# An attention and expert kernel on one core: the short chunk of the second pair moves to the end, and one PSUM bank is borrowed in the first twelve steps

## The chip, the core and the metric

The kernel runs on one core of a Trainium2 chip. The metric is device time in microseconds, the median of a few executions of the whole program, with nothing done on the host between. Lower is better. TensorE (PE), VectorE (DVE), ScalarE (ACT), GpSimd (POOL) and the DMA queue of SyncE (SP) each work through a list of instructions in order, and wait for each other by semaphores.

## What is computed

An attention with a learned position bias, then a two-layer network with squared ReLU on its output:

```python
scores = scale * np.matmul(q, k.transpose(0, 1, 3, 2))      # 4 batches, 8 heads, 576 positions, head width 64
x = (psi_rel / psi_i)[..., None]                            # from the positions alone
bias = np.maximum(x @ w1 + b1, 0.0) @ w2                    # hidden width 32, one value per head
scores = scores + bias.transpose(2, 0, 1)[None, :, :, :]
attn = softmax(scores)
y = np.matmul(attn, v)                                      # 2304 tokens of 512
h = np.maximum(y @ moe_w_in, 0.0)                           # 512 -> 2048
out = h * h @ moe_w_out                                     # 2048 -> 512
```

## The kernel before

**Pairs, chunks, steps.** The four batches are two pairs, p = 0 and 1. The 576 query rows of a batch are cut into five chunks: c = 1 to 4 have 128 rows for each of the two batches, 256 tokens in all; c = 0 is the short one, the last 64 rows of both batches, 128 tokens in all. A step is one pair, one chunk and one head, so there are 80 steps, eight to a chunk. `ORDER` (line 40) says in which order the chunks of each pair run. In the first pair the short chunk comes first. In the second pair it comes second, as steps 48 to 55; steps 56 to 79 are three full chunks.

**A step of attention.** `qk` (line 366) makes the scores in PSUM, `softmax_a` (393) adds the bias and takes the maximum on DVE (line 405, once for each batch of a full step, once in all for a short one) and the exponentials on ACT (line 411). `softmax_b` (414) brings the exponentials into the layout that the product with v needs. For the first two chunks of the first pair, steps 0 to 15, it does this with float32 transposes on PE: four blocks of 128 columns at line 423 for each batch, then the rest block of 64 columns at line 427, each into a PSUM bank that ACT copies out (lines 424 and 428). For all later steps ACT and POOL split the exponentials into two float16 parts (lines 436 to 438) and the DMA queue transposes them (440, `at<-a`). `pv` (446) is the product with v. It stands three steps behind in the program (`LAG`).

**Banks of PSUM.** The pool `ps_h` has two banks, tag `h`, and three kinds of user: the transposes of steps 0 to 15, the bias products `bp` (line 317) and the first-layer outputs `hp` (line 524). They take its banks in the order of the program. `ps_o` has one bank each for `o0` and `o1`, the second-layer outputs; the first four bias groups and the weight conversion (`ci`, bank `o1`) also use them.

**The network.** When the eight heads of a chunk are done, `finish_x` (492) scales and splits the rows and transposes them by DMA (`xt<-xh`), and puts eight units into a queue. A unit is `g1` (515): 24 matmuls at line 524, of 256 columns for a full chunk and 128 for the short one; then relu on ACT (530), a product on DVE (532), a cast on DVE or POOL (127 or 125) and a difference on POOL (534); and `g2` (537): 12 matmuls of 512 columns at line 547 for a full chunk, 6 for the short one. `g2` of a unit follows two units behind its `g1` (`GLAG`). A step takes one unit from the queue, or two if more than `BACKLOG` wait; after step 79 the rest of the queue drains.

**The order.** The order written in the program is a wish: the Tile scheduler orders the instructions of each engine by its own model of time, so that a change in one place can move neighbours too. The position bias is made during steps 0 to 31 (`hgen`, `bias_mm`), written to a table in DRAM (`biasd`) and read back for each step (`bt`). The weights are converted in the first 16 steps.

Of the kernel before, what the change touches and what calls it, by code (L numbers as in the profile page):

```python
# [8 lines left out]
F32 = mybir.dt.float32  # L9
# [27 lines left out]
HID = "122222222211111000"  # L37

W_AT = [3, 2, 2, 2, 2, 2, 2, 2, 2, 2, 2, 2, 2, 2, 2, 1]
ORDER = [[0, 3, 2, 4, 1], [1, 0, 4, 2, 3]]  # L40
LAG, GLAG = 3, 2
BACKLOG = 10
AHEAD = 3
# [6 lines left out]
def tile_attention_moe(  # L50
# [14 lines left out]
    def pool(name, bufs, **kw):  # L65
        return ctx.enter_context(tc.tile_pool(name=name, bufs=bufs, **kw))
# [23 lines left out]
    ps_h = pool("ps_h", 2, space=PS)  # L90
    ps_o = pool("ps_o", 1, space=PS)
# [22 lines left out]
    now = [0]  # L114
# [6 lines left out]
    def cast(eng, out, in_, scale=1.0):  # L121
        if eng == "A":
            nc.scalar.activation(out=out, in_=in_, func=AF.Copy, scale=scale)  # L123
        elif eng == "P":
            nc.gpsimd.tensor_scalar(out, in_, scale, 1.0, op0=ALU.mult, op1=ALU.mult)
        else:
            nc.vector.tensor_scalar(out, in_, scale, None, op0=ALU.mult)  # L127


    k_t, v_t, q_t, v32 = {}, {}, {}, {}  # L130
    f32c = [(0, c) for c in ORDER[0][:NF]]

    def as_f32(t):
        return t.rearrange("p a b -> p (a b)").bitcast(F32)
# [279 lines left out]
    def softmax_b(p, c, h):  # L414
        e = st_.pop((p, c, h))
        nb = 2 if c else 1
        if (p, c) in f32c:

            at = as_f32(at_p.tile([128, 20, 128], F16, tag="at", name="at")).rearrange("p (k i) -> p k i", i=128)
            for b in range(nb):  # L420
                tp = ps_h.tile([128, 512], F32, tag="h", name="tp")
                for k in range(4):
                    nc.tensor.transpose(tp[:, 128 * k:128 * k + 128], e[:, S * b + 128 * k:S * b + 128 * k + 128], ident)
                nc.scalar.activation(out=at[:, 4 * b:4 * b + 4, :], in_=tp.rearrange("p (k i) -> p k i", i=128), func=AF.Copy)
            tp = ps_h.tile([128, 512], F32, tag="h", name="tp")
            for b in range(nb):
                nc.tensor.transpose(tp[0:64, 128 * b:128 * b + 128], e[:, S * b + 512:S * b + 576], ident)
            nc.scalar.activation(out=at[0:64, 4 * nb:5 * nb, :], in_=tp[0:64, 0:128 * nb].rearrange("p (k i) -> p k i", i=128),
                                 func=AF.Copy)
            st_[p, c, h, "t"] = at  # L430
            return
        a = a_p.tile([128, 2304], F16, tag="a", name="a")

        ev = e[:, 0:nb * S].rearrange("p (b j) -> p b j", b=nb)
        av = a[:, 0:nb * 2 * S].rearrange("p (b j) -> p b j", b=nb)
        cast("A", av[:, :, 0:576], ev)
        nc.gpsimd.tensor_tensor(av[:, :, 576:640], ev[:, :, 512:576], av[:, :, 512:576], op=ALU.subtract)  # L437
        nc.gpsimd.tensor_tensor(av[:, :, 640:1152], ev[:, :, 0:512], av[:, :, 0:512], op=ALU.subtract)  # L438
        at = at_p.tile([128, 20, 128], F16, tag="at", name="at")
        nc.sync.dma_start_transpose(out=at[:, 0:9 * nb, :], in_=a[:, 0:nb * 2 * S])  # L440
        st_[p, c, h, "t"] = at
# [121 lines left out]

    order = [(p, c) for p in range(2) for c in ORDER[p]]
    steps = [(p, c, h) for p, c in order for h in range(H)]
# [169 lines left out]
    for t in range(NS + LAG):  # L735
# [5 lines left out]
        if t < NS:  # L741
            p, c, h = steps[t]
            qk(p, c, h)
            softmax_a(p, c, h)
            if t + 2 < NS:
                bias_ld(*steps[t + 2])
            if h % 4 == 2 and t + 2 < NS:
                q_split(*qlist[(t + 2) // 4])
                q_next()
            if len(moe) > BACKLOG:  # L750
                moe_unit()
            softmax_b(p, c, h)
            if last < 0 or steps[last][2] != H - 1:
                moe_unit()
# [74 lines left out]
```

## Time and profile before

| | us |
|---|---|
| median of 3 runs | 669.49 (669.07 to 672.53) |
| the profiled execution, its own time | 673.4 |
| its span, first to last instruction | 671.7 |
| PE busy | 618.1 (92%) |
| DVE busy | 409.6 (61%) |
| ACT busy | 384.9 (57%) |
| POOL busy | 376.4 (56%) |

The span has two parts. In the first 190 us no engine is full: the bias, the weights and the first steps share PE, DVE, ACT, POOL and the DMA engines. From there to the end PE is busy nearly all the time, apart from some short gaps. Busy shares over the whole span hide this; they are read for each stretch.

### The profile page before, as it was taken

What the parts mean: (1) busy time and instruction counts of PE and PEld (TensorE: products, weight loads), DVE (VectorE), ACT (ScalarE), POOL (GpSimd) and SP (SyncE); (2) the same over time, 40 slices, a digit from 0 to 9 for tenths busy, and PEclk for the clock granted to TensorE, in tenths of its full rate; (3) what the DMA queues carried; (4) which work ended last, traced back from release to release, by engine and by line L of the source; (5) the groups of instructions that cost most, each with busy time, mean ns of one, the idle gap of its engine ahead of it and who ended that gap; (6) DMA issues with size and microseconds to landing.
All of it is one profiled execution on the core that took longest, in us unless ns stands there. A gap on an engine that the chain in (4) does not pass through costs nothing.

```text
span 671.7 us, 15521 instructions
## 1 busy us (share of the span) xinstructions
PE 618.1 (92%) x6048; PEld 395.1 (59%) x6048; DVE 409.6 (61%) x809; ACT 384.9 (57%) x855; POOL 376.4 (56%) x391
## 2 busy tenths in 40 slices
PE   5676689899899999999999999999997999999997
PEld 2233356566455556765666766666664776676664
DVE  7787999898854864596676443446467546424111
ACT  5588789577865655645656532556666555521111
POOL 2665569798665455766675543455565554632221
PEclk9577889799999999999999999999997999999999
DMA  6999888576978777889978976557899678451000
GB/s 232 279 276 297 269 241 242 156 230 160 208 137 188 166 167 166 191 170 220 235 153 163 174 142 117 137 94 168 159 185 214 140 131 167 107 103 32 32 1 31
DMA packets 206568, 112.16 MB, mean 167 GB/s; under 512 B 167072, under 2 KB 183456, under 8 KB 206496
## 3 DMA queue, kind: packets, MB, share of 16 engines
q1 hardware_dynamic: 206496, 111.19, 72.3%
q8 instruction: 47, 0.77, 0.5%
q14 instruction: 25, 0.20, 0.1%
HBM read 55.44 MB, written 15.61 MB: 106 GB/s over the span
## 4 chain that ended last, share of the span: by engine, by line
PE 62%; DVE 11%; DMA 11%; ACT 5%; POOL 5%; issue 4%; SPq 0%; DVEq 0%; POOLq 0%; ACTq 0%
PE o L547 22%; PE hp L524 22%; PE pv L470 6%; DMA at<-a 5%; PE sc L389 4%; DVE hg L290 3%; PE bp L317 3%; DMA biasd<-be 2%; POOL a L438 2%; DVE s L405 2%; DMA bt<-biasd 1%; ACT s L411 1%; PE sc L383 1%; DVE ci L211 1%; PE sc L377 1%
## 5 line engine op out<-in xcount | busy, mean ns | idle before, releaser
L524 PE MATMUL hp<-xt,winH 128*128 128x256 f16 (+1 forms) x1280 | 196.0, 263 | 2.6 <-DMA xt<-xh 2.2
L547 PE MATMUL o<-woutH,g 128*128 128x512 f16 x576 | 185.9, 382 | 1.4 <-ACT o L554 0.8
L524 PE MATMUL hp<-xt,winL 128*128 128x256 f16 (+1 forms) x640 | 162.4, 262 | 0.0
L524 PEld LDWEIGHTS <-winH 128*128 128x128 f16 x1280 | 117.1, 98 | 36.1 <-issue 16.0
L547 PEld LDWEIGHTS <-g 128*128 128x128 f16 x864 | 82.8, 98 | 93.2 <-issue 9.1
L532 DVE TENSOR_TENSOR r<-hp,r 128x512 f32<-128x512 f32 (+1 forms) x80 | 50.7, 634 | 135.6 <-ACT r L530 135.5
L438 POOL TENSOR_TENSOR a<-s,a 128x1024 f16<-128x1024 f32 (+1 forms) x64 | 130.2, 2034 | 0.0
L534 POOL TENSOR_TENSOR g<-r,g 128x512 f16<-128x512 f32 (+1 forms) x80 | 86.0, 1075 | 78.5 <-DVE g L127 76.5
L405 DVE CUSTOM_DVE_ANT_0 s<-sc,bt 128x576 f32<-128x576 f32 x144 | 103.5, 751 | 31.7 <-PE sc L389 22.2
L411 ACT ACTIVATE s<-s,nm 128x576 f32<-128x576 f32 x144 | 111.4, 773 | 6.8
L547 PE MATMUL o<-woutL,g 128*128 128x512 f16 x288 | 109.9, 382 | 0.0
L437 POOL TENSOR_TENSOR a<-s,a 128x128 f16<-128x128 f32 (+1 forms) x64 | 28.8, 450 | 138.3 <-ACT a L123 126.3
L409 ACT ACTIVATE nm<-mx,esc 128x1 f32<-128x1 f32 x144 | 41.3, 287 | 108.2 <-DVE mx L405 108.0
L123 ACT ACTIVATE a<-s 128x1152 f16<-128x1152 f32 (+1 forms) x64 | 70.5, 1102 | 50.9 <-DMA at<-a 49.6
L470 PE MATMUL pv<-v,at 128*128 128x64 f16 (+5 forms) x2112 | 96.8, 208 | 1.5 <-DMA at<-a 1.1
L530 ACT ACTIVATE r<-hp 128x512 f32<-128x512 f32 (+1 forms) x80 | 43.1, 539 | 57.0 <-PE hp L524 56.0
L470 PEld LDWEIGHTS <-at 128*128 128x128 f16 (+1 forms) x1792 | 58.0, 100 | 21.1 <-issue 7.7
L290 DVE TENSOR_SCALAR hg<-tab_t,nb 128x528 f32<-128x528 f32 (+17 forms) x96 | 65.4, 729 | 7.1 <-PE bp L317 6.8
L524 PEld LDWEIGHTS <-winL 128*128 128x128 f16 x640 | 62.8, 98 | 6.2 <-issue 0.4
L317 PE MATMUL bp<-hg,w2s 128*32 128x288 f32 (+17 forms) x352 | 49.0, 544 | 7.1 <-ACT hg L287 3.7
L389 PE MATMUL sc<-k,q 64*128 64x512 f16 x384 | 54.7, 390 | 0.0
L127 DVE TENSOR_SCALAR g<-r 128x512 f16<-128x512 f32 (+1 forms) x61 | 37.2, 610 | 2.4
(72 smaller groups left out, 638.4 us busy)
## 6 DMA issues: line engine op xcount, KB each, us to landing
bt<-biasd SPq DMA_DIRECT2D x64, 288.0 KB, 3.2
stg<-w_in SPq DMA_DIRECT2D x16, 512.0 KB, 5.2
stg<-w_out SPq DMA_DIRECT2D x16, 512.0 KB, 4.9
bt<-biasd SPq DMA_DIRECT2D x32, 144.0 KB, 3.5
qst<-qd SPq DMA_DIRECT2D x32, 128.0 KB, 3.4
out<-o SPq DMA_DIRECT2D x16, 256.0 KB, 2.4
v<-vd SPq DMA_DIRECT2D x8, 320.0 KB, 6.2
stg<-vd SPq DMA_DIRECT2D x8, 320.0 KB, 4.0
```

Source lines behind the costliest of these rows:

```text
L123: nc.scalar.activation(out=out, in_=in_, func=AF.Copy, scale=scale)
L290: nc.vector.tensor_scalar(ht, tab_t[:, 0:dlen(G)], scl[:, n:n + 1], nb1, op0=ALU.mult, op1=ALU.max)
L317: nc.tensor.matmul(out=bp[32 * t:32 * t + 32, 0:d1 - d0], lhsT=w2s, rhs=ts_[t][:, d0:d1], start=True, stop=True, tile_position=(0, 32 * t))
L389: nc.tensor.matmul(out=sc[:, 1024 * b:1024 * b + 512], lhsT=qt[r, qz, qs], rhs=kt[r, z, 64 * b:64 * b + 512], start=(n == 0), stop=(n == 2 ...
L405: nc.vector.tensor_tensor_reduce(s[:, 576 * b:576 * b + 576], sc[:, 960 * sb:960 * sb + 576], bt, inv, -3.0e38, ALU.add, ALU.max, mx[:, b: ...
L411: nc.scalar.activation(out=sl, in_=sl, func=AF.Exp, bias=nm[:, b:b + 1], accum_out=su[:, h, b:b + 1])
L438: nc.gpsimd.tensor_tensor(av[:, :, 640:1152], ev[:, :, 0:512], av[:, :, 0:512], op=ALU.subtract)
L470: nc.tensor.matmul(out=dst, lhsT=lhsT, rhs=vt[r, 5 * b + blk, :] if f32 else vt[:, vz, 5 * b + blk, :], start=(n == 0), stop=(n == nt - 1) ...
L524: nc.tensor.matmul(out=hp[:, f * T:f * T + T].rearrange("p (b t) -> p b t", b=nb), lhsT=wt[:, k, c0:c0 + 128], rhs=xt[:, 0:nb, z * 4 + k, ...
L532: nc.vector.tensor_tensor(rr, hp[:, 0:2 * T], rr, op=ALU.mult)
L534: nc.gpsimd.tensor_tensor(g[:, 1, 0:2 * T], r[:, 0:2 * T], g[:, 0, 0:2 * T], op=ALU.subtract)
L547: nc.tensor.matmul(out=blk["o"][b], lhsT=g[:, z, c0:c0 + 128], rhs=wt[:, 2 * u + f, :], start=(u == 0 and f == 0 and z == 0 and wt is wout ...
```

## The change

`ORDER` of the second pair becomes [1, 4, 2, 3, 0]: the full chunks 4, 2 and 3 become steps 48 to 71, and the short chunk becomes steps 72 to 79. In steps 0 to 11 the rest blocks (line 427) are written to bank `o0` of `ps_o`; steps 12 to 15 use `ps_h` as before.

```diff
-ORDER = [[0, 3, 2, 4, 1], [1, 0, 4, 2, 3]]
+ORDER = [[0, 3, 2, 4, 1], [1, 4, 2, 3, 0]]
...
-            tp = ps_h.tile([128, 512], F32, tag="h", name="tp")
+            tp = ps_o.tile([128, 512], F32, tag="o0", name="tp") if now[0] < 12 else ps_h.tile([128, 512], F32, tag="h", name="tp")
             for b in range(nb):
                 nc.tensor.transpose(tp[0:64, 128 * b:128 * b + 128], e[:, S * b + 512:S * b + 576], ident)
```

No instruction is added or taken away; what moves is shown at three places.

DVE, step 66, before: the second maximum of the step (`s,mx`), then the end of a full chunk (`x`, `ax`, `cc`, `xh`), with the product `r<-hp` and the cast `g<-r` of one unit in between.

```order
L405 ISA s,mx<-sc,bt 128x576
L405 ISA mx 128x1
L482 TENSOR_TENSOR x<-pv,rd 128x256 x2
L499 TENSOR_REDUCE ax<-x 128x2
L532 TENSOR_TENSOR r<-hp,r 128x256
L501 TENSOR_SCALAR ax<-ax 128x1 x2
L127 TENSOR_SCALAR g<-r 128x256
L502 RECIPROCAL cc<-ax 128x2
L507 TENSOR_SCALAR xh<-x,cc 128x512
L508 SCALAR_TENSOR_TENSOR xh<-x,cc,xh 128x512
```

The same step in the changed kernel:

```order
L405 ISA s,mx<-sc,bt 128x576
L405 ISA mx 128x1
L482 TENSOR_TENSOR x<-pv,rd 128x256 x2
L499 TENSOR_REDUCE ax<-x 128x2
L501 TENSOR_SCALAR ax<-ax 128x1 x2
L502 RECIPROCAL cc<-ax 128x2
L507 TENSOR_SCALAR xh<-x,cc 128x512
L508 SCALAR_TENSOR_TENSOR xh<-x,cc,xh 128x512
L532 TENSOR_TENSOR r<-hp,r 128x512
```

The unit beside this step is one of the short chunk before (256 wide) and one of a full chunk now (512 wide). It is so in each of the steps 61 to 68.

ACT, the end of the program, before: the last step's exponentials, then relus of the units and the copies of the two output banks.

```order
L411 ACTIVATE s,sum<-s,nm 128x576
L530 ACTIVATE r<-hp 128x512
L123 ACTIVATE a<-s 128x2x576
L479 ACTIVATE rd<-sum,eps 128x8
L530 ACTIVATE r<-hp 128x512 x2
L503 ACTIVATE os<-ax 128x2
L530 ACTIVATE r<-hp 128x512 x5
L554 ACTIVATE o<-o_8525,os 128x512
L554 ACTIVATE o<-o_8526,os 128x512
L530 ACTIVATE r<-hp 128x512 x6
L554 ACTIVATE o<-o_9012,os 128x512
L554 ACTIVATE o<-o_9013,os 128x512
```

The same end in the changed kernel:

```order
L411 ACTIVATE s,sum<-s,nm 128x576
L479 ACTIVATE rd<-sum,eps 128x4
L123 ACTIVATE a<-s 128x576
L530 ACTIVATE r<-hp 128x512 x3
L503 ACTIVATE os<-ax 128x1
L530 ACTIVATE r<-hp 128x512 x3
L530 ACTIVATE r<-hp 128x256 x2
L554 ACTIVATE o<-o_8582,os 128x512
L554 ACTIVATE o<-o_8583,os 128x512
L530 ACTIVATE r<-hp 128x256 x6
L554 ACTIVATE o<-o_9063,os 128x512
```

The eight short units now stand at the very end, after all attention, and the last block has one output bank instead of two.

PE, after the scores of step 9, before: the transposes of step 8 (x8, both batches), its rest blocks, a bias product, the first transposes of step 9.

```order
L389 MATMUL sc<-k,q 128x512
L423 MATMUL tp<-ident,s 128x128 x8
L470 MATMUL pv<-v,at 128x64 x4
L427 MATMUL tp<-ident,s 64x128 x2
L317 MATMUL bp<-hg,w2s 32x400 x4
L423 MATMUL tp<-ident,s 128x128 x4
L470 MATMUL pv<-v,at 128x64 x6
```

The same place in the changed kernel:

```order
L389 MATMUL sc<-k,q 128x512
L423 MATMUL tp<-ident,s 128x128 x4
L427 MATMUL tp<-ident,s 64x128 x2
L423 MATMUL tp<-ident,s 128x128 x4
L470 MATMUL pv<-v,at 128x64 x5
L317 MATMUL bp<-hg,w2s 32x400 x4
L423 MATMUL tp<-ident,s 128x128 x4
L470 MATMUL pv<-v,at 128x64 x5
```

The rest blocks at line 427 in this piece are now those of step 9, not of step 8, and stand ahead of the second half of step 8's transposes and of the bias product. Steps 9 to 11 show the same.

## Rows read from the trace of the kernel before

**Rows 1.** Stretches: start:end, length, busy of PE, PEld, DVE, ACT, POOL, PEclk, DMA, GB/s.

```profile
0.00:190.00 190.00, 149.19 (x1267) 87.56 (x1267) 160.03 (x296) 142.53 (x328) 132.49 (x158) 0.87 0.83 231
190.00:471.46 281.46, 277.91 (x2877) 179.68 (x2875) 164.23 (x329) 156.66 (x345) 159.06 (x160) 1.00 0.80 165
471.46:519.92 48.46, 42.91 (x567) 27.84 (x566) 30.48 (x68) 32.06 (x74) 28.18 (x28) 0.93 0.94 190
519.92:668.10 148.18, 148.07 (x1345) 100.01 (x1342) 54.83 (x116) 52.97 (x108) 56.68 (x48) 1.00 0.41 82
...
384.00:436.80 52.80, 52.80 (x558) 35.12 (x556) 22.59 (x48) 20.61 (x47) 24.62 (x29) 1.00 0.68 135
```

**Rows 2.** Chain of waits, 400 to 512 us: start, length, what; first-layer matmuls by step.

```profile
410.17 2.62 PE hp L524 x24
...
416.78 2.62 PE hp L524 x24
...
464.48 2.73 PE hp L524 x24
467.20 2.59 PE o L547 x12
...
471.53 1.45 PE hp L524 x24
...
483.08 1.45 PE hp L524 x24
...
487.56 1.13 PE hp L524 x19
488.68 6.46 DMA at<-a
```

**Rows 3.** PE in order of time, 462 to 521 us: start, length, instruction, idle before.

```profile
506.41 0.33 PE L383 MATMUL sc<-kz,q 128*128 128x128 f16 x3 [0.47 <-DVE mx L405]
...
507.42 0.28 PE L524 MATMUL hp<-xt,winH 128*128 128x128 f16 x2
...
514.98 0.48 PE L383 MATMUL sc<-kz,q 128*128 128x128 f16 x3 [3.94 <-DVE mx L405]
...
516.79 0.61 PE L547 MATMUL o<-woutH,g 128*128 128x512 f16 x1
...
519.92 0.38 PE L524 MATMUL hp<-xt,winH 128*128 128x256 f16 x2
```

**Rows 4.** Line 524, 471 to 512 us: weight loads of short units, ns min/median/max.

```profile
L524 PEld LDWEIGHTS <-winH x128: 95/98/99, 471.5 to 508.6; 128*128 128x128 f16 x128
```

**Rows 5.** ACT and POOL, 470 to 516 us: first and last work on a short unit.

```profile
473.63 0.36 ACT L530 ACTIVATE r<-hp 128x256 f32<-128x256 f32 x1
...
474.92 0.67 POOL L534 TENSOR_TENSOR g<-r,g 128x256 f16<-128x256 f32 x1 [1.73 <-DVE g L127]
```

**Rows 6.** The end: the last copy on ACT; issue times of the short chunk's stores, ns.

```profile
668.11 0.69 ACT L554 ACTIVATE o<-o,os 128x512 f32<-128x512 f32 x1 [0.18 <-PE o L547]
L561 SPq DMA_DIRECT2D out<-o x4: 545/569/589, 193.2 to 532.5; - x4
```

**Rows 7.** DVE's waits, 20 to 115 us.

```profile
DVE hg L290 <- PE bp L317: 1.7, 3, 1.2
...
DVE s L405 <- PE tp L423: 0.9, 1, 0.9
...
DVE s L405 <- PE tp L427: 0.6, 1, 0.6
```

**Rows 8.** The page, costliest groups: the two ACT operations before an exponential is ready.

```profile
L411 ACT ACTIVATE s<-s,nm 128x576 f32<-128x576 f32 x144 | 111.4, 773 | 6.8
...
L409 ACT ACTIVATE nm<-mx,esc 128x1 f32<-128x1 f32 x144 | 41.3, 287 | 108.2 <-DVE mx L405 108.0
```

**Rows 9.** Chain of waits, 14 to 135 us: bias written to and read from DRAM.

```profile
38.75 5.31 DMA bt<-biasd
...
49.79 5.95 DMA biasd<-be
```

## The prediction

> **What bounds the kernel now.** The busy times of the page come first: PE is by far the fullest engine, but the mean over the span hides stages, so I cut the span into stretches [rows 1]. In the first 190 us PE works 149.2 us, and DVE is the fullest engine with 160.0; no engine is full, so here waits count. From 190 to 471.46 us PE is busy for 277.9 of 281.5 us. From 471.46 to 519.92 it works only 42.9 of 48.5 us, at a lower mean clock (0.93). From 519.92 to 668.1 it is full again (148.07 of 148.18) [rows 1]. So after 190 us a microsecond counts if it is one of PE's gaps, and 5.55 us of them (48.46 less 42.91) lie in one stretch of 48 us.
>
> The chain of waits tells what that stretch is [rows 2]. The distance from one unit's first-layer matmuls to the next is PE's work in one step: 6.61 us for a short step with a full unit (410.17 to 416.78), 7.05 us for a full step with a full unit (464.48 to 471.53), and 4.48 us for a full step with a short unit (483.08 to 487.56). The eight short units, those of 1.45 us, run beside the full steps 61 to 68. Right after 487.56 the chain leaves PE for a transposing DMA of 6.46 us [rows 2]: with 4.48 us of work in a step PE overtakes the attention chain (exponentials, split, transposition), which needs more than that for a full step. The largest gap, 3.94 us, is PE waiting for the maximum of step 68 before it may write the scores of step 69 [rows 3]. The granted clock falls behind it: the same two groups of score matmuls take 1.01 us before the gap (506.41 to 507.42) and 1.81 us after it (514.98 to 516.79), and the 4.94 us up to 519.92 run near 1.2 GHz instead of 2.4 [rows 3].
>
> **The change, part by part: the order of the chunks.** Steps 48 to 55 become full, steps 72 to 79 short, and the short units leave the full steps: they become the last eight units of the drain, where no attention runs. Each kind of work keeps its count, so PE's sum does not change; only its gaps can.
>
> Removed: the 5.55 us of gaps, and the slow clock behind them. 4.94 us at the slow level hold 2.47 us of work at the fast one if the ratio is two, 2.76 us if it is the 1.81 to 1.01 of the rows; the excess is 2.2 to 2.5 us, and I take 2.3. Together 7.85 us. What is late next in these steps is PE itself: a full unit beside a full step is 7.05 us of PE work, and PE had no gap worth naming with such steps after 519.92 us [rows 1].
>
> Moved into the new place: each short step issues its two bias loads and one transposition on SP, two loads and two memsets for q per four steps (SP and POOL), one DVE maximum and one exponential instead of two. They now go past the stores of full chunks on SP, as they did in steps 48 to 55. There 6.61 us of PE work in a step covered them [rows 2], and PE was busy for all of the 52.8 us of these steps [rows 1]; the cover is the same full unit, now in steps 72 to 79. If the cover were gone, the price is that of one transposition, 6.46 us [rows 2].
>
> The drain: a short unit is 1.45 us of first-layer work and half of a full unit's second layer, 1.3 of 2.59 us [rows 2]. Its way from relu to the last difference took 1.96 us (473.63 to 475.59) [rows 5], with other work between. At the very end two second layers of short units, 2.6 us, are all that is left on PE between the last first layer and its second. So the chain of a unit stays hidden, and I cost it at nothing; uncovered, it would cost up to 1.96 us once.
>
> Added: the last block is stored as two DMAs of 64 rows instead of one of 128. The issue of one takes 0.57 us on SP [rows 6], so the second starts 0.57 us later than the single store that follows the last copy at 668.11 us now: +0.57.
>
> **The rest blocks in bank o0.** In steps 0 to 11 one user leaves the two `h` banks. DVE decides how fast these steps go, so I count only what DVE waits for PE there: 1.7 us for the bias product that frees its buffer, 0.9 and 0.6 us for scores behind transposes, 3.2 us in all from 20 to 115 us [rows 7]. That is the most this part can give, and only if nothing else comes last; the other waits of DVE there are for DMAs and POOL. Against it stands the order that the scheduler made: in steps 8 to 11 the rest blocks of a step now stand on PE ahead of the second half of the previous step's transposes and ahead of a bias product, so these wait for the exponentials of the newer step. Two exponentials with their small first operation are 2 x (0.773 + 0.287) = 2.1 us [rows 8]. Queued behind them are the product with v and the bias product, and for the latter DVE waits with its next bias rows. Four such steps cost at most 8.5 us. The bank `o0` itself is free then: its next user is the second layer of the first unit, at step 13. The trace of before cannot show which of both wins. DVE has the same number of instructions ahead of each maximum within a few, and conversions of weights to fill a wait, so I take 0, between -3.2 and +8.5, nearer to the first end.
>
> **A rule against the change.** The weight loads of the short units take 98 ns each [rows 4], and 24 matmuls took 1.45 us [rows 2], 60 ns apiece: the loads overlapped. The Trainium skill (TensorE: Matmul & The Clock Gate, section Back-to-back issue gap) gives about 81 ns per matmul for a stream of weight loads and matmuls of 128 columns. By that figure, as an estimate, a short unit in a drain of nothing else would take 1.94 us instead of 1.45, eight of them 3.9 us more, and the forecast would be 666.1; the trace disagrees with it beside attention, and no run here yet shows the drain.
>
> **The sum.** -5.55 - 2.3 + 0.57 + 0 = -7.3 us. Against the profiled execution's own 673.4 that is 666.1. That execution is 3.9 us longer than the median; taken from the median of 669.49, the same 7.3 us give 662.2.
>
> **The rivals.** One: the front gains too: 3.2 us more, 659.0. For it: every one of those waits is on a bank or on PE's order. Against it: DVE's other waits there.
>
> Two: the 3.94 us gap belongs to the profiled execution. It is 3.9 us over the median, and this is the largest gap of PE after 190 us. Then the timed runs have only 1.61 us of gaps there to lose and no slow clock, and gain 1.61 - 0.57 = 1.04: 668.4. Against it: 4.48 us of work in a step lets PE run dry in any execution.
>
> Three: the short units are paced by their weight loads where nothing else runs: 24 x 98 ns = 2.35 us instead of 1.45, eight times 0.9 = 7.2 us: 669.4. Against it: the rows of short units are already back to back within a unit.
>
> Four: the front loses the whole 8.5 us: 670.7. It decides if DVE has nothing to do while the bias product is late.
>
> Five: the front loses a round trip of the bias table, the case on the slow side: a bias product that is late by a step is stored late, and the load of the next step's bias waits for it in DRAM. One store and one load, uncovered, are 5.95 + 5.31 = 11.3 us [rows 9]: 673.5. It decides from the point where the store comes later than the load's turn on SP; the bias is made up to three steps ahead, which speaks against it.
>
> **How the numbers follow.** Forecast 0.64, with a range of its own from 659.0 to 664.3 (the front between -3.2 and one step's 2.1); the front gains 0.14; the gap is the profile's 0.08; paced by weight loads 0.03; 8.5 us lost 0.06; round trip 0.05. Half a per cent, about what a measurement of this kernel can tell from no change, is 3.3 us: faster means under 666.1, slower over 672.8. Faster is 0.64 + 0.14 = 0.78; same is 0.08 + 0.03 + 0.06 = 0.17; slower is 0.05. The range takes in the forecast, the front's gain (659.0, less 0.4 for what runs differ below the median) and the profile's gap: 658.6 to 668.4, which holds 0.86.
>
> **What would show it.** Right: PE without a gap of over 1 us and with a granted clock of 1.00 from about 460 us to the drain; the steps 61 to 68 at 7.05 us of PE work each; eight units of 1.3 to 1.5 us at the end; two stores of 64 rows last. Wrong: PE waiting for `mx` or `at` in steps 61 to 79, short units in the drain over 1.5 us in their first layer, or a front whose step 16 comes later than before, with DVE waiting for `bp` or for `biasd` between 70 and 125 us.

## The result and the profile after

| | before | after |
|---|---|---|
| median | 670.62 us (669.07 to 672.53, 6 executions) | 662.86 us (660.17 to 666.75, 6 executions) |
| ratio, with its 95% interval | | 0.9889 (0.9849 to 0.9929) |
| the profiled execution, its own time and span | 673.4, 671.7 | 666.75, 664.8 |
| PE busy | 618.1 | 614.5 |

The change made the kernel 7.8 us faster; the interval allows 4.8 to 10.1 us. Every ratio here leaves out the slow executions, those more than 1.5% above the fastest of their kernel; of the kernel with the short chunk third, below, that leaves three of seven, of the first run with the bank in eight steps three of six, so these two ratios are the weakest.

The first view is the table of stretches of the changed kernel, with the columns of [rows 1].

```profile
0.00:190.00 190.00, 146.93 (x1242) 88.15 (x1243) 161.01 (x295) 140.97 (x324) 129.70 (x156) 0.87 0.81 229
190.00:470.00 280.00, 277.33 (x2863) 179.63 (x2861) 170.75 (x345) 167.03 (x365) 166.17 (x155) 1.00 0.82 173
470.00:520.00 50.00, 50.00 (x519) 33.58 (x518) 24.13 (x57) 28.90 (x62) 26.45 (x24) 1.00 0.81 157
520.00:661.00 141.00, 140.27 (x1432) 94.30 (x1429) 53.81 (x114) 49.38 (x105) 53.45 (x58) 1.00 0.43 85
```

The third line answers to the third of [rows 1]. Where PE had 5.55 us of gaps and a mean clock of 0.93, it is now busy for all of the 50 us, at 1.00. The first line answers to the first: the front has still no full engine.

The second view is PE's waits of the changed kernel from 190 us to the end: who waited for whom, us in total, times, longest.

```profile
PE hp L524 <- DMA xt<-xh: 1.5, 1, 1.5
PE o L547 <- ACT o L554: 0.6, 1, 0.6
PE sc L383 <- DVE mx L405: 0.6, 1, 0.6
```

The wait for the maximum that took 3.94 us at once [rows 3] is gone; the 0.6 us that is left of this kind lies far ahead of it. From 460 us on no wait is listed at all.

The third view is the chain of waits, in the full steps and the short steps of the second pair and in the drain: start, length, what.

```profile
469.10 2.73 PE hp L524 x24
471.83 2.59 PE o L547 x12
...
476.15 2.73 PE hp L524 x24
...
483.21 2.73 PE hp L524 x24
...
580.46 2.62 PE hp L524 x24
...
587.08 2.62 PE hp L524 x24
...
649.78 1.34 PE hp L524 x24
651.12 1.29 PE o L547 x6
652.41 1.34 PE hp L524 x24
653.75 1.29 PE o L547 x6
655.05 1.34 PE hp L524 x24
656.39 3.90 PE o L547 x18
660.28 0.02 issue
660.31 0.02 ACTq L554
660.32 0.04 issue
660.37 0.69 ACT o L554
```

Full steps with a full unit follow each other at 7.05 us (469.10, 476.15, 483.21), the short steps at 6.61 us (580.46 to 587.08), and in the whole view no piece of another engine stands between: PE is what the program waits for from 400 us to 660.28. At the end stand the short units, 1.34 us of first layer and 1.29 us of second, back to back.

### The profile page after: what moved, and what is told of

Its sections match the earlier page's. It is cut to its first block, busy times and chain, and to the rows that moved or that the text cites. A ratio compares the mean times of both kernels' runs of the same rounds, so it can differ in the third digit from the quotient of the medians.

```text
span 664.8 us, 15541 instructions
## 1 busy us (share of the span) xinstructions
PE 614.5 (92%) x6048; PEld 395.7 (60%) x6048; DVE 409.7 (62%) x809; ACT 386.3 (58%) x855; POOL 375.8 (57%) x391
## 4 chain that ended last, share of the span: by engine, by line
PE 67%; DMA 9%; DVE 8%; POOL 7%; ACT 4%; issue 4%; SPq 0%; DVEq 0%; POOLq 0%; ACTq 0%
PE hp L524 23%; PE o L547 23%; PE pv L470 8%; PE sc L389 5%; PE bp L317 4%; DMA at<-a 2%; DVE hg L290 2%; POOL a L438 2%; DMA kst<-kd 2%; PE sc L383 1%; PE sc L377 1%; DMA stg<-w_out 1%; DVE s L405 1%; PE tp L423 1%; ACT s L411 1%
## 5 line engine op out<-in xcount | busy, mean ns | idle before, releaser
L290 DVE TENSOR_SCALAR hg<-tab_t,nb 128x528 f32<-128x528 f32 (+17 forms) x96 | 67.9, 756 | 8.4 <-PE bp L317 8.3
L317 PE MATMUL bp<-hg,w2s 128*32 128x288 f32 (+17 forms) x352 | 46.7, 545 | 9.3 <-ACT hg L287 4.3
L470 PEld LDWEIGHTS pv<-v,at 128*64 128x64 f32 (+3 forms) x320 | 31.6, 191 | 14.8 <-issue 10.0
```

Of the source, the lines that this page charges most:

```text
L290: nc.vector.tensor_scalar(ht, tab_t[:, 0:dlen(G)], scl[:, n:n + 1], nb1, op0=ALU.mult, op1=ALU.max)
L317: nc.tensor.matmul(out=bp[32 * t:32 * t + 32, 0:d1 - d0], lhsT=w2s, rhs=ts_[t][:, d0:d1], start=True, stop=True, tile_position=(0, 32 * t))
L470: nc.tensor.matmul(out=dst, lhsT=lhsT, rhs=vt[r, 5 * b + blk, :] if f32 else vt[:, vz, 5 * b + blk, :], start=(n == 0), stop=(n == nt - 1) ...
```

## The experiments

Eleven runs were made, in three groups on three chips; three of them repeat a kernel. The kernel before ran beside each group, so every ratio is to its own neighbours. Two readings are used for all of them. One is the ratio of the timed executions. The other cuts the span of the profiled execution at the first maximum of step 24 (line 405, read from the timeline of DVE), when the weights and the float32 transposes are over: what comes ahead is the front, what follows is the rest. The last bias products (line 317) reach into the rest, to about 250 us.

| kernel | front, us | rest, us | median of all executions, us | ratio to before |
|---|---|---|---|---|
| before | 207.25 | 464.45 | 670.62 to 673.59 | |
| changed | 209.20 | 455.60 | 662.86 | 0.9889 (0.9849 to 0.9929) |
| changed, second run | 208.35 | 455.15 | 664.16 | 0.9874 (0.9844 to 0.9905) |
| changed, third run | 209.45 | 455.35 | 663.53 | 0.9879 (0.9840 to 0.9919) |
| order alone | 210.04 | 456.56 | 666.73 | 0.9912 (0.9881 to 0.9943) |
| bank alone | 209.64 | 461.56 | 672.91 | 0.9998 (0.9965 to 1.0031) |
| short chunk third | 206.74 | 459.06 | 675.04 | 0.9928 (0.9901 to 0.9956) |
| short chunk fourth | 212.04 | 462.26 | 672.46 | 0.9980 (0.9942 to 1.0017) |
| short first layers doubled, old order | 204.83 | 467.57 | 675.77 | 1.0086 (1.0045 to 1.0127) |
| short first layers doubled, new order | 213.53 | 467.07 | 675.56 | 1.0043 (1.0007 to 1.0078) |
| bank in 8 steps | 205.28 | 455.82 | 671.59 | 0.9897 (0.9829 to 0.9964) |
| bank in 8 steps, second run | 205.93 | 456.57 | 667.77 | 0.9937 (0.9900 to 0.9974) |
| bank in 8 steps, bias products doubled | 211.00 | 455.10 | 664.32 | 0.9900 (0.9866 to 0.9934) |

The rest tells the orders apart: 455.1 to 456.6 us in all seven profiles that have the short chunk last and no work added behind step 24. With the old order there are two, 464.45 and 461.56 us, so a rest of that order is known to no better than 2.9 us. The front moves by up to 8.7 us between profiles and does not go by order or bank.

### The order alone

```diff
-ORDER = [[0, 3, 2, 4, 1], [1, 0, 4, 2, 3]]
+ORDER = [[0, 3, 2, 4, 1], [1, 4, 2, 3, 0]]
```

> Only the order of the chunks is changed (the short chunk last in the second pair); the rest blocks keep the two h banks. Gap theory (PE runs dry where short units stand beside full steps, and the clock falls behind it): the whole gain is here, about 7.3 us, ratio near 0.989, PE without a gap over 1 us from 470 us to the drain. Rival (the bank carries part of it): a ratio of 0.993 or more.

Measured: 0.9912 (0.9881 to 0.9943). The order alone holds most of the gain; its rest of 456.56 us is 7.9 us shorter than before's. The interval reaches over the rival's 0.993, so the run of the bank alone has to decide between the two.

### The bank alone

```diff
-            tp = ps_h.tile([128, 512], F32, tag="h", name="tp")
+            tp = ps_o.tile([128, 512], F32, tag="o0", name="tp") if now[0] < 12 else ps_h.tile([128, 512], F32, tag="h", name="tp")
```

> Only the bank of the rest blocks in steps 0 to 11 is changed; the chunks keep their old order. Gap theory: the stall near steps 65 to 69 stays, and the front moves by 0 to +2 us (step 21 came 2.9 us later in the changed kernel's trace than before), ratio 1.000 to 1.003. Rival (the bank relieves the front): 3.2 us faster, ratio 0.995.

Measured: 0.9998 (0.9965 to 1.0031), no difference; the rival's 0.995 lies outside. Its profile also answers the rival that the large gap belonged to one execution. PE in order of time, with the idle time before in brackets:

```profile
506.84 0.33 PE L383 MATMUL sc<-kz,q 128*128 128x128 f16 x3 [0.49 <-DVE mx L405]
515.19 0.43 PE L383 MATMUL sc<-kz,q 128*128 128x128 f16 x3 [3.71 <-DVE mx L405]
```

In another execution, of another program with the same order of chunks, the same matmuls wait at the same step, for 3.71 us where before they waited 3.94 [rows 3]. The gap belongs to the old order. The slow clock behind it is less constant: the mean clock of 460 to 530 us is 0.98 here and 0.95 in before's profile, and the rest of this kernel is 2.9 us shorter than before's.

What PE waits for there is shown by the chain of waits of the kernel before, just ahead of the gap:

```profile
506.25 3.09 DMA xt<-xh
...
509.37 0.03 DVE xh L507
...
510.97 2.60 DVE xh L508
513.58 0.67 DVE s L405
```

It is the end of a full chunk: its rows are scaled on DVE and transposed in two halves, both through the one buffer that the pool of `xh` has (line 81). DVE scales the second half only when the 3.09 us transposition of the first is over, and the maxima of step 68 stand behind that in its list. In the bank alone the same transposition, of 3.07 us, stands ahead of the 3.71 us.

### Both, again

No diff: this is the changed kernel beside the two halves.

> The changed kernel once more, on the same chip as the two halves. If the parts add up, its ratio is the product of theirs; gap theory: 0.989 to 0.992. Rival (the parts help each other): clearly below the product.

Measured: 0.9874 (0.9844 to 0.9905). The product of the halves is 0.9912 x 0.9998 = 0.9910, which lies within the noise of the three: the halves can explain the whole, and what the bank adds beside the order, if anything, is below what these runs can tell.

### The short chunk third

```diff
-ORDER = [[0, 3, 2, 4, 1], [1, 0, 4, 2, 3]]
+ORDER = [[0, 3, 2, 4, 1], [1, 4, 0, 2, 3]]
```

> The short chunk third in the second pair: [1, 4, 0, 2, 3]. Its units stand beside full steps again, eight steps later (69 to 76). Gap theory: the gaps move with them, PE waits for mx or at between about 545 and 580 us and none at 500, time within 2 us of before, ratio 0.997 to 1.003. Rival (something at this place of the program, such as its DMA traffic, makes the gap): no gap, ratio 0.989.

Measured: 0.9928 (0.9901 to 0.9956), a gain where none was expected; but it rests on three executions, and the median of all seven, 675.04 us, lies above before's 671.73. The profile tells more. The eight short units stand beside full steps here too, one chunk later, and PE runs dry there:

```profile
566.97 0.33 PE L383 MATMUL sc<-kz,q 128*128 128x128 f16 x3 [1.94 <-DVE mx L405]
569.62 0.39 PE L524 MATMUL hp<-xt,winH 128*128 128x256 f16 x2 [0.82 <-DMA xt<-xh]
```

The gap moved with the short units, but it is 2.76 us (1.94 + 0.82) and not 5.55, and the clock stays at 1.00 behind it. Ahead of the 1.94 us DVE waits again for the transposition of a chunk's first half:

```profile
564.28 0.49 DVE L507 TENSOR_SCALAR xh<-x,cc 128x512 f16<-128x512 f32 x1 [2.46 <-DMA xt<-xh]
```

So the place of the gap is right and the expected price was not. The rest is 459.06 us: 2.5 us longer than that of the order alone, about this gap, and 2.5 to 5.4 us shorter than the two of the old order.

### The short chunk fourth

```diff
-ORDER = [[0, 3, 2, 4, 1], [1, 0, 4, 2, 3]]
+ORDER = [[0, 3, 2, 4, 1], [1, 4, 2, 0, 3]]
```

> Only the order of the chunks is changed: the short chunk of the second pair is fourth of five, so its eight units begin five steps into the last full chunk: some three of them run beside full steps, the others in the drain after all attention. Theory (PE runs dry because eight short units in a row stand beside full steps): three short units in a row do not let PE overtake the attention far enough, PE's gaps after 190 us stay under 1.5 us apart from waits for xt, the clock stays at 1.00, and the time is that of the kernel with the order alone, 0.989 to 0.993 of before. Rival (any short unit beside a full step gives the gap): one gap of 1 to 3 us, 0.993 to 1.000.

Measured: 0.9980 (0.9942 to 1.0017). Both theories are off, since the loss is elsewhere. The chain of waits at the end of the attention:

```profile
595.14 1.45 PE hp L524 x24
...
604.55 6.18 DMA at<-a
...
619.70 3.09 DMA xt<-xh
...
624.11 3.07 DMA xt<-xh
...
627.32 9.50 PE hp L524 x72
```

And the stretches (columns as in [rows 1]):

```profile
600.00:627.00 27.00, 23.03 (x313) 16.18 (x310) 11.61 (x29) 6.86 (x17) 9.06 (x10) 1.00 0.56 106
627.00:640.00 13.00, 12.69 (x91) 9.62 (x92) 3.35 (x6) 2.37 (x4) 3.45 (x3) 0.87 0.09 21
```

Three short units run beside the last full steps without a gap, as expected. But after them only five short units are left in the queue when the last scores are done, and the way of that chunk from its last transposition through scaling to the two transposing DMAs of its tokens, one behind the other, is longer than their work. PE idles for 3.97 us up to 627.00 (27.00 less 23.03) and for 0.3 more up to 627.32, and the mean clock of the next 13 us is 0.87: the chain has 72 first-layer matmuls in 9.50 us, where three full units at 2.62 us need 7.86. Together about 5.9 us, and the rest is 5.7 us longer than that of the order alone (462.26 against 456.56). A short chunk last has a second use, which the prediction did not name: in the changed kernel three full units with their second layers are still in the queue when the last product with v is done (618.27 us), and PE has 15.7 us of work until the first short unit at 634.01.

### The short first layers doubled, in both orders

```diff
-        for f in range(2):
+        for f in [0, 0, 1, 1] if blk["p"] and not blk["c"] else [0, 1]:
```

The first layer of the second pair's short units is computed twice, to the same values. The first kernel has the old order, the second one the new order of the chunks beside this edit.

> The order of before; the first layer of the eight short units of the second pair is computed twice, with the same result, so PE has 8 x 1.34 to 1.45 = 10.7 to 11.6 us more matmul work, beside the full steps 61 to 68. Theory (PE has 5.55 us of gaps there and a slow clock behind them, because 4.48 us of work in a step is less than the attention needs): the added work fills the gaps first, PE's gaps of 470 to 520 us fall under 2 us, and the time rises by 3 to 6 us only, 1.005 to 1.009. Rival (the gaps have another cause, or are the profile's alone): the whole 10.7 to 11.6 us is added, 1.015 to 1.018.

> The changed order without the bank, and the same doubling: the first layer of the eight short units of the second pair, now in the drain, is computed twice. PE is full there, so both theories expect the whole added work: 8 x 1.34 = 10.7 us over the kernel with the order alone, 1.005 to 1.009 of before, 1.016 of the order alone. It measures what the added work costs where nothing can hide it, beside the kernel that does the same among the full steps. If less than 8 us comes, the drain has gaps of its own.

Measured: 1.0086 (1.0045 to 1.0127) in the old order, which is 5.8 us of before's 673.6, where some 10.7 us of work were added; 1.0043 (1.0007 to 1.0078) in the new order, a little under what was expected; over the 0.9912 of the order alone it is 0.0131, or 8.8 us. These two costs have intervals of about 3 us to either side, so the executions alone do not part 5.8 from 8.8. In the profiles' rests, one each, the same edit costs 3.1 us in the old order (467.57 less 464.45; 6.0 against the 461.56 of the bank alone) and 10.5 us in the new (467.07 less 456.56). The stretch of the old order with the doubled layers:

```profile
471.00:520.00 49.00, 47.74 (x708) 35.26 (x706) 24.31 (x61) 28.16 (x65) 23.55 (x23) 1.00 0.84 162
```

PE has 1.26 us of gaps left (49.00 less 47.74), and the clock is 1.00. The added work fell into the gaps, and with them filled the clock did not fall. DVE still waits here for the transposition of a chunk's first half, for 2.91 us at 513.81, but PE has work meanwhile. With the gaps filled the two orders take nearly the same time (rests 467.57 and 467.07, medians 675.77 and 675.56, ratios with overlapping intervals): as far as these runs can tell, the gain of the new order was these gaps and the clock behind them. In the drain the doubled layers take their full price:

```profile
653.62 2.68 PE hp L524 x48
656.30 1.29 PE o L547 x6
657.60 2.68 PE hp L524 x48
```

48 matmuls in 2.68 us are 56 ns apiece, twice the 1.34 us of a short unit in the changed kernel's drain.

### The bank in eight steps, twice, and with filling

```diff
-            tp = ps_o.tile([128, 512], F32, tag="o0", name="tp") if now[0] < 12 else ps_h.tile([128, 512], F32, tag="h", name="tp")
+            tp = ps_o.tile([128, 512], F32, tag="o0", name="tp") if now[0] < 8 else ps_h.tile([128, 512], F32, tag="h", name="tp")
```

This was tried as a version better than the changed kernel, since in three profiles with the bank in twelve steps the early gain was lost in steps 10 to 13.

> The changed kernel with the rest blocks in bank o0 in steps 0 to 7 only; in steps 8 to 11 they use the pool of before. Theory A (the bank gains 2 to 5 us in steps 1 to 10 and loses 3 to 6 us in steps 11 to 13, because the rest blocks of steps 8 to 11 wait for the newer exponentials ahead of older work): the loss is gone, steps 11 to 16 begin 2 to 4 us earlier than in the changed kernel, and the time falls by up to 2 us, 0.984 to 0.988 of before. Theory B (DVE has conversions of weights that must be done by step 16 in any case, so a gain before it is refilled): step 16 begins within 1 us of before, and the time is that of the changed kernel, 0.987 to 0.990.

Measured: 0.9897 (0.9829 to 0.9964). Its profile began steps 11 and 16 5.8 and 1.5 us earlier than the changed kernel's, which leans to theory A, but its times were no better. So it ran again, beside the changed kernel and a third version, in which the four matmuls of each bias product of steps 9 to 11 are issued twice, to the same values:

```diff
-            for t in range(4):
+            for t in [0, 1, 2, 3] * (2 if 9 <= now[0] < 12 else 1):
```

> The changed kernel with the rest blocks in bank o0 in steps 0 to 7 only, a second time, beside the changed kernel itself. Theory (what the bank gives up to step 10 is lost in the stretch of 105 to 115 us, in which PE is full at half the granted clock, whether or not the rest blocks of steps 8 to 11 stand ahead of older work): the time is that of the changed kernel within 0.4%, and the profile has such a stretch again. Rival (the order of steps 8 to 11 cost the gain): 1.5 to 3 us less than the changed kernel, 0.996 of it.

> As the kernel with the bank in steps 0 to 7, with the four matmuls of each bias product of steps 9 to 11 issued twice, with the same result: 3 x 0.83 = 2.5 us more work for PE, next to the place where PE waited 1.4 us for ACT ahead of the stretch at half clock. Theory (the clock falls behind that wait and takes 4 to 5 us): the wait shrinks, the clock stays at 1.00 in 104 to 114 us and the time falls by 2 to 4 us against the kernel without the filling. Rival (the clock in the first 130 us falls for other reasons, or the work is on the path): 1 to 3 us more, and the stretch at half clock is still there.

> The changed kernel a third time, to be compared with the two others of this call: 0.987 to 0.990 of before by all theories. Its profile tells whether the stretch at half clock between 104 and 120 us belongs to the kernel or to single executions: theory that it belongs to the kernel: PE full at a granted clock of 0.50 to 0.65 in at least two of the stretches 105-110, 110-115 and 115-120; rival: 0.9 or more in these.

Measured: 0.9937 (0.9900 to 0.9974) for eight steps, 0.9900 (0.9866 to 0.9934) with filling, 0.9879 (0.9840 to 0.9919) for the changed kernel. No version beats it. That the order of steps 8 to 11 cost the bank's gain falls: without it the kernel is not faster, by its medians rather slower (0.6%, more than the 0.4% that was expected at most). What both share is a stretch at half the clock. The changed kernel's third run, then the first and the second run of the bank in eight steps, columns as in [rows 1]:

```profile
100.00:105.00 5.00, 1.72 (x15) 1.12 (x15) 4.64 (x10) 2.42 (x6) 4.77 (x7) 0.98 0.77 267
105.00:120.00 15.00, 14.41 (x74) 10.17 (x71) 11.74 (x23) 11.13 (x27) 12.15 (x14) 0.50 0.69 213
```

```profile
85.00:100.00 15.00, 13.74 (x94) 9.35 (x94) 14.60 (x28) 12.95 (x32) 10.33 (x13) 0.81 0.95 254
100.00:120.00 20.00, 17.40 (x118) 12.54 (x114) 16.95 (x32) 14.47 (x35) 16.27 (x19) 0.74 0.61 183
```

```profile
85.00:100.00 15.00, 14.63 (x69) 9.79 (x69) 10.68 (x21) 9.29 (x21) 8.97 (x11) 0.50 0.83 222
100.00:120.00 20.00, 17.08 (x143) 11.81 (x139) 19.50 (x36) 17.73 (x43) 17.20 (x21) 0.93 0.70 205
```

In the changed kernel's third run PE has only 1.72 us of work from 100 to 105 us and then works 15 us at a clock of 0.50, nearly full; all its three profiles and that of the bank alone show PE at 0.50 to 0.65 in each 5 us from 105 to 120. In the kernel with eight steps the place differs between two executions of the same program, on two chips. The filling did not hold the clock: its profile has PE at 0.50 from 80 to 115 us, 31.81 us busy of 35. Its median is 3.5 us under that of the eight steps without filling, which is the time its theory asked for, but the ratios' intervals overlap and the reason of the theory, a clock held at 1.00, did not come.

## Why the prediction held, step by step

**What bounds the kernel.** Right: from 190 us on PE does, outside its gaps. The doubled layers show it: by the profiles the same added work cost 3.1 us (6.0 against the other profile of the old order) beside the full steps of the old order and 10.5 us in the drain. Rival two, that the gap was the profiled execution's own, falls with the 3.71 us of the bank alone.

**The gaps and the clock, -7.85.** Right that PE runs dry where short units stand beside full steps; right only in part on what it then waits for. The prediction names exponentials, split and transposition of a step. The 3.94 us end with the close of a chunk: a 3.09 us transposition of its first half, then DVE's scaling of the second, then the maxima. From the first scaling of the chunk to the end of step 68's maxima DVE took 11.7 us (503.23 to 514.9) in the kernel before, and 12.5 us (515.42 to 527.9) at the same place of the changed one. This lasts two steps of PE, which have 9.0 us of work at 4.48 us and 14.1 at 7.05: the change hides this chain and does not shorten it. Whether a second `xh` buffer would close the gap in the old order, no run shows. The size of the term was read from one execution, and that it came out so near is partly luck. Against before's profile the rests of the kernels with the new order are 7.9 to 9.4 us shorter, against that of the bank alone, which has the old order, 5.0 to 6.5 us. The granted clock behind the gap differs between those two (0.95 and 0.98 from 460 to 530 us). PE's waits from 190 us on fell by 6.3 us between the profiles of before and after, from 9.0 to 2.7: the 5.55 of the sum and some small ones.

**The cover of the short steps, 0.** Right: 6.61 us from unit to unit four times in a row in the short steps (573.85 to 600.30 us), as predicted from steps 48 to 55 [rows 2], and no wait of PE there. The full steps 61 to 68 are 7.05 us apart, as said.

**The drain, 0.** Right. The prediction took 1.45 us for a short unit's first layer; it is 1.34 us. The way of a short unit from its relu to its difference, on ACT and POOL:

```profile
653.84 0.38 ACT L530 ACTIVATE r<-hp 128x256 f32<-128x256 f32 x1 [2.25 <-PE hp L524]
...
655.22 0.67 POOL L534 TENSOR_TENSOR g<-r,g 128x256 f16<-128x256 f32 x1 [2.01 <-DVE g L127]
```

This is 2.05 us (653.84 to 655.89), against 1.96 taken, and it lies beside two units of 2.63 us. Rival three, units paced by their weight loads at 2.35 us, falls. The rule of about 81 ns per matmul of 128 columns (the Trainium skill, TensorE: Matmul & The Clock Gate, section Back-to-back issue gap) is not borne out here: 1.34 us for 24 matmuls are 56 ns apiece, in a stretch with no attention beside it.

**The second store, +0.57.** Somewhat more. From the start of the last copy to the end of the span it was 3.59 us before (668.11 to 671.7 [rows 6]) and is 4.43 us now (660.37 to 664.8): +0.84.

**The bank, 0 between -3.2 and +8.5.** The value was right within the 0.3% of the run of the bank alone, the reasons for its bounds only in part. The gain was said to be 3.2 us of DVE's waits for PE; steps 5 to 10 did begin 0.9 to 4.6 us earlier in the changed kernel, but DVE's wait for the bias product [rows 7] grew, from 1.7 to 2.7 us (line 290, four waits). The loss was said to come from rest blocks that wait for newer exponentials; PE waited only 0.8 us in all for that (line 427 behind line 411, from 14 to 135 us). PE's waits changed their kind: those for copies of the transposes (lines 424 and 428) fell from 11.1 to 5.3 us between 20 and 135 us, and those for maxima ahead of the scores rose from 3.3 to 9.0 us. The loss of 6.2 us between steps 10 and 13 (from 2.0 us earlier to 4.2 later than before) lies where PE works at half the clock, and that was no term of the sum. By step 16 it is given back but for 0.4 us; the prediction's reason for that, DVE's conversions that fill its waits, is not tested by itself. A step 16 later than before, with DVE waiting for the bias product between 70 and 125 us (2.2 us in two waits, none before), is in small what the prediction named as a sign of being wrong; the order alone, without the bank, began step 16 later still (145.33 us). That the new order of PE's work brings the clock down there is not shown; the runs show the slow stretch between 105 and 120 us in four profiles of four with the bank in twelve steps, and in two of the six without the bank. Rivals one, four and five fall: the bank neither gains 3.2 us nor costs 8.5 by its ratio (0.9998), and no wait for `biasd` grew to a round trip (DVE's waits for it are 1.3 us in all from 20 to 115 us).

**The total.** The prediction took its 7.3 us from the first three executions' median of 669.49; with six the median is 670.62, and 7.8 us were gained.

## What to carry to other kernels

Where two chains run side by side and the fuller engine's work per step varies, do not compare the sums: compare each step's work on that engine with the time that the other chain needs for that step, the closing step of a chunk above all, and place the light pieces where the other chain is over. Look also at what stands in the queue when the last chain ends, since that work must cover the chain's last latencies; moving the small piece to the place before the last one lost nearly all of the gain here (0.9980 against 0.9912). To see what idle time is worth, add work into it that changes no result, and the same work where the engine is full: the difference is the slack, clock included.

## What the hardware showed that was not expected

TensorE can be full and stay at the lower clock, here for 30 us. In the profile of the new order with doubled layers:

```profile
60.00:90.00 30.00, 19.79 (x173) 10.11 (x170) 28.08 (x53) 23.53 (x56) 16.40 (x18) 0.81 0.87 260
90.00:120.00 30.00, 30.00 (x136) 19.16 (x136) 21.07 (x40) 18.83 (x45) 18.85 (x23) 0.50 0.67 194
120.00:150.00 30.00, 26.47 (x234) 19.37 (x233) 26.26 (x49) 22.28 (x52) 25.86 (x34) 0.95 0.61 194
```

PE is busy for 30.00 of 30 us at 0.50, which is 1.2 GHz, after 30 us in which it was busy for 19.79. The kernel with the order alone, whose program is the same but for the doubled layers at the end, had 0.91 there, on another chip. One group of work at both levels:

```profile
101.37 1.51 PE L317 MATMUL bp<-hg,w2s 128*32 128x384 f32 x8
```

In the changed kernel the same eight matmuls take 0.85 us at 98.78 us, where the clock is 1.00. This execution began step 16 at 150.58 us and that of the order alone at 145.33, so 5.3 us of the difference between the two come from the front. Executions of one kernel differ by some 6 us and more in most groups here (the changed kernel: 659.63 to 666.75), about as much as the change is worth, which is why a profile's total alone does not tell kernels of this size of difference apart, and the rest behind step 24 does so better. Why the clock stays low in the front while the engine is full, and not from 190 us on, no run here settles.
